# Attention and gated MoE on one core: a first chunk of four q-tiles, and the split of work between VectorE and GpSimd

## The chip, the cores and the metric

One core of a Trainium2 chip. The metric is the device time of one execution in microseconds. The kernel before took 841.29 us (median of three runs, 840.37 to 841.69). Engines are named as in the profile: PE is TensorE, DVE is VectorE, ACT is ScalarE, POOL is GpSimd, SP is SyncE, which issues most DMAs.

## What is computed

```python
def _attn_ref(q, k, v, n_sink, window):          # B, H, S, D = 4, 8, 768, 64; n_sink 4, window 128
   scores = scale * np.matmul(q, k.transpose(0, 1, 3, 2))
   rel = pos[:, None] - pos[None, :]
   keep = is_sink | ((rel >= 0) & (rel < window))
   scores = np.where(keep, scores, -1000000000.0)
   a = np.exp(scores - np.max(scores, axis=-1, keepdims=True))
   a = a / (np.sum(a, axis=-1, keepdims=True) + 1e-09)
   return np.matmul(a, v).astype(np.float32)

def _moe_ref(x, w_a, w_b, w_out):                # x 3072x512, w_a and w_b 512x1536, w_out 1536x512
   return ((x @ w_a) * (x @ w_b) @ w_out).astype(np.float32)
```

The attention's output, heads side by side, is x. The three weights come as float64.

## The kernel before

**Tiles and chunks.** A q-tile is 128 rows of one batch; there are 24. With a window of 128 and a few sink keys, q-tile t needs only key block t, block t - 1 and the sinks, so its scores are 128x264 (128x128 for t = 0, which has no block before it). The work goes in chunks of three q-tiles: `(b, t0, 3)` for pairs of batches, t0 = 0 and then 3. For each chunk there is an attention (8 heads x 3 tiles = 24 units) and then an MoE over the chunk's 384 rows.

**Stages.** `run` first does the attention of chunk 0 with nothing beside it (`alone=True`). Then, for each chunk, `moe` runs and the attention of the next chunk is drawn in beside it step by step: `attention` returns a generator, and `between(s)` takes as many of its steps as keep it evenly spread over the MoE's 36 thirds. The last chunk's MoE has no attention beside it.

**The MoE.** For each of 12 column blocks j: product a (`half("a", j)`), copied out by ACT as g (L670); product b, multiplied with g on DVE (L674); g is split into gh (ACT, L677) and gl (GpSimd, L679); then the output product of the block before (`project`, L662). Every float32 factor is used as an exact pair of parts, high and low (float32r), with three matmuls a product: 12 matmuls of n = 384 columns for a and for b, 9 of 512 columns for the output. PSUM banks: a, b, o0 to o2 for three outputs, and s, t, av for the attention.

**Weights.** Each of 36 weight tiles is loaded as float64 words and split on the core: two bit operations on DVE (L279, L284), a scaling of the low words on ACT (L283; on GpSimd for the first five, L281), a sum on GpSimd (L286), the high part on ACT (L293), and the low part on DVE (L298; on GpSimd for the first five). `weights_to` does one step of this pipeline: the bit operations of weight k, the high part of k - 3 (`D1`) and the low part of k - 4 (`D2`). These steps are taken from step 17 (`STEP0`) of the first attention on, at every second one (`STEPS`), and then once in each third of the first MoE. Loads run nine tiles ahead (`LOADS`).

**Attention.** The first two chunks use `parts_exact`, on float32 operands as they are; later ones use `parts_split`, with K, Q and V split into two parts by GpSimd (L326, L329). A unit: scores on PE; mask and maximum on DVE (L535); exp and sum on ACT (L537); two small DVE operations for the reciprocal (L539, L540); scaling of the probabilities, on DVE in the first attention (L542), on ACT in the others; transposes on PE (L564, L565) and a copy on ACT (L566); and once a head the product with V (L578). The transposes follow the scores by 3 units in the first attention and by 2 in the others. In the second attention K and Q of heads 3, 5 and 7 are split as in later ones (`SPLIT_KQ`).

**Order.** Each engine executes its instructions in order. The framework's planner chooses that order; instructions pinned with `keep_in_program_order` keep theirs among each other. Nearly all loads are on SP's queue, the outputs on ACT's (the last on SP's).

Of the kernel before, what the change touches and what calls it, by code (L numbers as in the profile page):

```python
# [19 lines left out]
P = 128  # L20
# [166 lines left out]
# Where a q-tile's transposed probabilities go (first slot, second slot, own block B before or after A),  # L187
# and the products of V with them: (key block, first slot, step of slots, first column tile). A lone slot
# (step 0) goes in with its two parts side by side, the low one's product into the fourth column tile.
UNITS = ((0, 4, "BA"), (1, 2, "AB"), (3, 5, "AB"))  # L190
GROUPS = ((0, 0, 1, 0), (2, 5, 0, 2), (-1, 4, 2, 0), (1, 2, 1, 1))


class Fast:
# [37 lines left out]
    def masks(self, val):  # L232
        """What is added to the scores: 0 where a key is kept, -NEG where it is not."""
# [37 lines left out]
    def early(self, kind, j):  # L271
        return 3 * j + "abo".index(kind) < POOL_FIRST

    def weight_bits(self, kind, j):
# [5 lines left out]
        if self.early(kind, j):  # L280
            nc.gpsimd.tensor_scalar(lo, lo.bitcast(U32), 2.0 ** -29, 1.0, op0=ALU.mult, op1=ALU.mult)  # L281
        else:
            pin(nc.scalar.activation(lo, lo.bitcast(U32), AF.Copy, scale=2.0 ** -29))  # L283
# [11 lines left out]
    def weight_low(self, kind, j):  # L295
        wh, wl = self.wt[kind, j]
        e = self.nc.gpsimd if self.early(kind, j) else self.nc.vector
        i = e.tensor_tensor(wl, self.wf.pop((kind, j)), wh.bitcast(F32), op=ALU.subtract)  # L298
# [73 lines left out]
    def attention(self, b, t0, nt, xf, exact=False, split=(), alone=False):  # L372
        parts = self.parts_exact(b, t0, nt, xf, split, alone) if exact else self.parts_split(b, t0, nt, xf)
# [107 lines left out]
    def parts_exact(self, b, t0, nt, xf, split, alone):  # L481
        """On float32 operands as they are (but K and Q of heads in `split`): more passes of the tensor engine."""
# [7 lines left out]
        preps, state, sc, vss, pts, skt = {}, {}, {}, {}, {}, {}  # L490

        def do_prep(h):
# [3 lines left out]
            if h in split:  # L496
                kq = self.prep_kq(b, h, t0, nt)
            else:
                if alone and h % 2:
                    k = self.io([P, MK], F32, f"kx{u}")  # L500
                else:
                    k = self.sp.tile([P, MK], F32, tag="ks", name=f"kx{u}")
                nc.sync.dma_start(k[:, :kw], self.kD[b, h, :, s0 * KB:s0 * KB + kw])
                q = self.sp.tile([P, 3 * P], F32, tag=("qh", "ql")[h % 2], name=f"qx{u}")
                nc.sync.dma_start(q[:, :nt * P], self.qT[b, h, :, t0 * P:(t0 + nt) * P])
                kq = k, q
            if h % 2 == 0:
                v = self.sp.tile([P, 2, 4, D], F32, tag="vv", name=f"vx{u}")
                nc.sync.dma_start(v[:, :, :nb], self.vB[b, h // 2, :, :, s0:s0 + nb])
            else:  # L510
                v = preps[h - 1][1]
            preps[h] = kq, v
            if h % 2 == 0 and late:
                vs = self.sp.tile([2 * NS, P], F32, tag="vs", name=f"vsx{u}")
                nc.sync.dma_start(vs, self.vS[b, h // 2, :2 * NS])
                vss[h // 2] = vs

        def scores(h, i):
            k, *qs = preps[h][0]
# [6 lines left out]
            for m, q in enumerate(qs):  # L526
                nc.tensor.matmul(ps[:, :w], lhsT=q[:, i * P:(i + 1) * P], rhs=k[:, c0:c0 + w],  # L527
                                 start=m == 0, stop=m == len(qs) - 1)
# [6 lines left out]
            nc.vector.tensor_tensor_reduce(out=p[:, :w], in0=ps[:, :w], in1=m, scale=-0.0625 * len(qs), scalar=BIG,  # L535
# [5 lines left out]
            if alone:  # L541
                nc.vector.tensor_scalar(p[:, :w], p[:, :w], st[:, 3:4], None, op0=ALU.mult)  # L542
# [3 lines left out]
            if i in late:  # L546
                if h % 2 == 0:
                    sc[h // 2, i] = self.at.tile([P, 2, NS], F32, tag=f"sc{i}", name=f"sc{u}", bufs=2)
                nc.vector.tensor_copy(sc[h // 2, i][:, h % 2, :], p[:, P:P + NS])

        def transposes(h, i):
# [5 lines left out]
            pt = pts[0][:, h % 2]  # L557
            n = units.index((h, i))
            tp = self.ps.tile([P, 2, P], F32, tag="tb"[n % 2] if alone else "t", name=f"t{u}")
            if t == 0:  # L560
                nc.tensor.transpose(tp[:, 1, :], p[:, :P], self.ident)
                nc.scalar.copy(pt[:, 1, :], tp[:, 1, :])
                return
            nc.tensor.transpose(tp[:, 0, :], p[:, :P], self.ident)  # L564
            nc.tensor.transpose(tp[:, 1, :], p[:, P + NS:], self.ident)  # L565
            nc.scalar.copy(pt[:, 2 * i:2 * i + 2, :], tp)  # L566

        def av(h):
            v = preps[h][1][:, h % 2]
            ps = self.ps.tile([P, 3 * P], F32, tag="av", name=f"av{tag}_{h}")  # L570
            rows = slice(0, D) if h % 2 == 0 else slice(D, P)
            pt = pts[0][:, h % 2]
            for i in range(nt):
                blks = [(t0 + i - s0, 2 * i + 1)]
                if t0 + i:
                    blks.append((t0 + i - 1 - s0, 2 * i))
                for k, (blk, sl) in enumerate(blks):
                    nc.tensor.matmul(ps[rows, i * P:(i + 1) * P], lhsT=v[:, blk, :], rhs=pt[:, sl, :],  # L578
                                     start=k == 0, stop=k == len(blks) - 1)
            nc.scalar.copy(xf[h // 2][rows, :nt * P], ps[rows, :nt * P])  # L580

        def sinks_t(pr):
            n = len(late)
            tp = self.ps.tile([2 * NS, 3 * P], F32, tag="t", name=f"skt{tag}_{pr}")
            for k, i in enumerate(late):
                nc.tensor.transpose(tp[:, k * P:(k + 1) * P], sc[pr, i].rearrange("p a b -> p (a b)"), self.ident)
            s = self.at.tile([2 * NS, 3 * P], F32, tag="sct", name=f"sct{tag}_{pr}", bufs=1)
            nc.vector.tensor_copy(s[:, :n * P], tp[:, :n * P])
            skt[pr] = s

        def sinks_av(pr):
            n = len(late)
            ps = self.ps.tile([P, 3 * P], F32, tag="av", name=f"sk{tag}_{pr}")
            nc.tensor.matmul(ps[:, :n * P], lhsT=vss[pr], rhs=skt.pop(pr)[:, :n * P], start=True, stop=True)
            xs = xf[pr][:, late[0] * P:nt * P]
            nc.vector.tensor_tensor(xs, ps[:, :n * P], xs, op=ALU.add)
# [3 lines left out]
    def pipeline(self, units, nt, late, do_prep, scores, transposes, av, sinks_t, sinks_av, lag):  # L600
        do_prep(0)
        yield
        nu = len(units)
        for k in range(nu + lag + 3):
            if k < nu:
                h, i = units[k]
                if i == 0:
                    do_prep(h + 1)
# [18 lines left out]
    def split_x(self, xf, nt, tag):  # L627
# [11 lines left out]
    def moe(self, row, nt, xf, between, weights_ahead, last):  # L639
# [26 lines left out]
        for j in range(NJ):  # L666
            weights_ahead(3 * j)
            pa = half("a", j)
            g = self.mo.tile([P, 3 * P], F32, tag="g", name=f"g{tag}_{j}", bufs=1)
# [5 lines left out]
            gh = self.mo.tile([P, 3 * P], F32R, tag="gh", name=f"gh{tag}_{j}")  # L675
            gl = self.mo.tile([P, 3 * P], F32R, tag="gl", name=f"gl{tag}_{j}")
# [19 lines left out]
    def run(self, scalars):  # L696
        chunks = [(b, t0, 3) for b0 in range(0, B, 2) for t0 in (0, 3) for b in (b0, b0 + 1)]
# [15 lines left out]
        xf = self.new_xf(0)  # L713
# [134 lines left out]
```

## Time and profile before

| | before |
|---|---|
| runs (us) | 841.69, 841.29, 840.37; median 841.29 |
| the profiled execution | span 839.9 us from the first to the last instruction |
| busy | PE 800.4 (95%), DVE 503.1 (60%), ACT 461.9 (55%), POOL 398.9 (47%) |
| first attention | 0 to about 44 us |
| first MoE chunk | about 44 to 174.5 us |
| six chunks with an attention of three tiles beside them | 98.7, 98.3, 93.9, 93.9, 98.5, 99.4 us |
| last chunk, and what follows it | 75.1 and 7.6 us |
| mean granted TensorE clock | 0.981 |

How to read the views: a row of stretches gives the stretch, its length, the busy time and number of instructions of each engine, the granted TensorE clock, the DMA engines' busy share and GB/s. A row of waits gives who waited for whom, the total, how often, and the longest. A row of a line gives its instructions with least, median and greatest duration in nanoseconds. A row of the timeline gives start and duration.

### The profile page before, as it was taken

What the parts mean: (1) busy time and instruction counts of PE and PEld (TensorE: products, weight loads), DVE (VectorE), ACT (ScalarE), POOL (GpSimd) and SP (SyncE); (2) the same over time, 40 slices, a digit from 0 to 9 for tenths busy, and PEclk for the clock granted to TensorE, in tenths of its full rate; (3) what the DMA queues carried; (4) which work ended last, traced back from release to release, by engine and by line L of the source; (5) the groups of instructions that cost most, each with busy time, mean ns of one, the idle gap of its engine ahead of it and who ended that gap; (6) DMA issues with size and microseconds to landing.
All of it is one profiled execution on the core that took longest, in us unless ns stands there. A gap on an engine that the chain in (4) does not pass through costs nothing.

```text
span 839.9 us, 13792 instructions
## 1 busy us (share of the span) xinstructions
PE 800.4 (95%) x4481; PEld 722.7 (86%) x4481; DVE 503.1 (60%) x1648; ACT 461.9 (55%) x1291; POOL 398.9 (47%) x493
## 2 busy tenths in 40 slices
PE   8977887999999999999999999999999999999996
PEld 5666776989998899999999999998999898999995
DVE  6999998555765576745656365646676567550101
ACT  5657666555554566645755466645665566542111
POOL 2375776835654365624555265624656346401110
PEclk9989999899999999999999999999999999999998
DMA  8944620321211133222333133321343113001001
GB/s 290 322 169 185 229 76 20 97 70 33 58 36 51 51 100 119 88 93 61 103 103 94 53 94 112 98 96 63 98 122 94 62 57 98 1 1 38 1 1 42
DMA packets 44977, 75.11 MB, mean 89 GB/s; under 512 B 4832, under 2 KB 25952, under 8 KB 44896
## 3 DMA queue, kind: packets, MB, share of 16 engines
q1 hardware_dynamic: 41840, 68.63, 25.9%
q10 hardware_dynamic: 3024, 5.51, 1.8%
q8 instruction: 37, 0.61, 0.3%
q14 instruction: 44, 0.36, 0.1%
q0 software_dynamic: 32, 0.00, 0.0%
HBM read 67.83 MB, written 6.29 MB: 88 GB/s over the span
## 4 chain that ended last, share of the span: by engine, by line
PE 77%; DVE 16%; ACT 4%; issue 2%; DMA 0%; ACTq 0%; DVEq 0%; POOLq 0%
PE o L662 22%; PE b L653 20%; PE a L653 20%; PE t L435 4%; PE av L451 4%; DVE sc L417 2%; PE s L399 2%; PE s L400 2%; DVE wf_b L279 1%; PE av L578 1%; DVE w_o L298 1%; DVE wf_a L279 1%; PE s L527 1%; DVE wf_b L284 1%; DVE wf_a L284 1%
## 5 line engine op out<-in xcount | busy, mean ns | idle before, releaser
L653 PE MATMUL a<-xh,w_a 128*128 128x384 f32 x768 | 221.4, 349 | 0.2 <-DVE st L535 0.2
L653 PE MATMUL b<-xh,w_b 128*128 128x384 f32 x768 | 218.3, 345 | 0.0
L679 POOL TENSOR_TENSOR gl<-g,gh 128x384 fp32r<-128x384 f32 x88 | 91.7, 1042 | 218.0 <-ACT gh L677 216.9
L662 PE MATMUL o<-w_o,gh 128*128 128x512 f32 x576 | 187.4, 407 | 0.0
L653 PEld LDWEIGHTS a<-xh,w_a 128*128 128x128 f32 x768 | 143.0, 192 | 2.2 <-DVE st L535 0.5
L653 PEld LDWEIGHTS b<-xh,w_b 128*128 128x128 f32 x768 | 141.1, 190 | 0.4 <-issue 0.2
L653 PE MATMUL a<-xl,w_a 128*128 128x384 f32 x384 | 131.0, 341 | 2.0 <-DVE xl L635 2.0
L653 PE MATMUL b<-xl,w_b 128*128 128x384 f32 x384 | 129.9, 338 | 0.0
L674 DVE TENSOR_TENSOR g<-b,g 128x384 f32<-128x384 f32 x96 | 53.1, 554 | 121.0 <-PE b L653 118.8
L662 PEld LDWEIGHTS o<-w_o,gh 128*128 128x128 f32 x576 | 104.1, 190 | 19.5 <-issue 0.7
L662 PE MATMUL o<-w_o,gl 128*128 128x512 f32 x288 | 114.3, 397 | 0.0
L670 ACT COPY g<-a 128x384 f32<-128x384 f32 x96 | 45.3, 472 | 89.6 <-PE a L653 86.3
L410 ACT ACTIVATE p<-p,st 128x264 f32<-128x264 f32 (+1 forms) x144 | 72.3, 502 | 40.2 <-DVE st L409 40.2
L677 ACT CAST gh<-g 128x384 fp32r<-128x384 f32 x96 | 49.3, 513 | 79.9 <-DVE g L674 79.6
L406 ACT ACTIVATE p<-p,st 128x264 f32<-128x264 f32 (+1 forms) x144 | 72.6, 504 | 33.1 <-DVE st L404 33.1
L653 PEld LDWEIGHTS a<-xl,w_a 128*128 128x128 f32 x384 | 73.9, 192 | 3.8 <-DVE xl L635 2.3
L653 PEld LDWEIGHTS b<-xl,w_b 128*128 128x128 f32 x384 | 73.3, 191 | 0.0
L417 DVE CAST sc<-p 128x16 fp32r<-128x16 f32 x112 | 54.3, 485 | 30.8 <-ACT p L410 29.5
L438 ACT CAST pt<-t 128x256 fp32r<-128x256 f32 (+1 forms) x144 | 51.2, 356 | 39.0 <-PE t L435 38.3
L439 DVE TENSOR_TENSOR pt<-t,pt 128x256 fp32r<-128x256 f32 (+1 forms) x144 | 58.0, 403 | 20.7 <-ACT pt L438 19.7
L404 DVE CUSTOM_DVE_ANT_0 p<-s,mg 128x264 f32<-128x264 f32 x112 | 47.7, 426 | 35.9 <-PE s L400 35.6
L326 POOL TENSOR_SCALAR qh<-qr 128x384 fp32r<-128x384 f32 x51 | 27.1, 531 | 88.1 <-PE s L399 63.9
(142 smaller groups left out, 1419.7 us busy)
## 6 DMA issues: line engine op xcount, KB each, us to landing
qr<-in_qT_dram SPq DMA_DIRECT2D x51, 192.0 KB, 2.4
raw_a<-in_wa_dram SPq DMA_DIRECT2D x12, 512.0 KB, 6.5
raw_b<-in_wb_dram SPq DMA_DIRECT2D x12, 512.0 KB, 6.6
raw_o<-in_wo_dram SPq DMA_DIRECT2D x12, 512.0 KB, 5.6
chk_a<-in_wa_dram SPq DMA_DIRECT2D x24, 256.0 KB, 2.7
chk_b<-in_wb_dram SPq DMA_DIRECT2D x24, 256.0 KB, 2.9
chk_o<-in_wo_dram SPq DMA_DIRECT2D x24, 256.0 KB, 2.8
out_dram<-os ACTq DMA_DIRECT2D x21, 256.0 KB, 2.1
```

What stands on the lines that cost most here:

```text
L404: nc.vector.tensor_tensor_reduce(out=p[:, :w], in0=ps[:, :w], in1=m, scale=-0.125, scalar=BIG, op0=ALU.add, op1=ALU.min, accum_out=st[:, 0:1])
L406: nc.scalar.activation(p[:, :w], p[:, :w], AF.Exp, bias=st[:, 0:1], scale=-1.0, accum_out=st[:, 1:2])
L410: nc.scalar.mul(p[:, :w], p[:, :w], st[:, 3:4])
L417: nc.vector.tensor_copy(c[:, :, 0, h % 2, :], sk)
L438: nc.scalar.copy(hs, tp[:, :n, :])
L439: nc.vector.tensor_tensor(ls, tp[:, :n, :], hs.bitcast(F32), op=ALU.subtract)
L653: nc.tensor.matmul(ps[:, :n], lhsT=w[:, ksl], rhs=x[:, :n], start=kk == 0 and i == 0, stop=kk == NK - 1 and i == 2)
L662: nc.tensor.matmul(outs[i], lhsT=g[:, sl], rhs=w, start=j == 0 and k == 0, stop=j == NJ - 1 and k == 2)
L670: nc.scalar.copy(g[:, :n], pa[:, :n])
L674: nc.vector.tensor_tensor(g[:, :n], pb[:, :n], g[:, :n], op=ALU.mult)
L677: nc.scalar.copy(gh[:, :n], g[:, :n])
L679: e.tensor_tensor(gl[:, :n], g[:, :n], gh[:, :n].bitcast(F32), op=ALU.subtract)
```

## The change

The chunks are now one of four q-tiles, one of the other two of the same batch, and six of three:

```diff
+CHUNKS = ((0, 0, 4), (0, 4, 2), (1, 0, 3), (2, 0, 3), (1, 3, 3), (2, 3, 3), (3, 0, 3), (3, 3, 3))
...
-        chunks = [(b, t0, 3) for b0 in range(0, B, 2) for t0 in (0, 3) for b in (b0, b0 + 1)]
+        chunks = CHUNKS
```

So the first attention has 32 units, the second (tiles 4 and 5 of batch 0) 16. The first MoE has 512 columns, the second 256; the fourth output of the first takes the bank av, so the second attention shares one bank between transposes and products (`half_bank`). The outputs are staged in the buffers of gh and gl instead of three of their own:

```diff
+        def half_bank(second, name):
+            if not bank:
+                bank[0] = self.ps.tile([P, 4, P], F32, tag="t", name=name)
+            return bank[0][:, 2:] if second else bank[0][:, :2]
...
-        outs = [self.ps.tile([P, DM], F32, tag=f"o{i}", name=f"o{tag}_{i}") for i in range(nt)]
+        outs = [self.ps.tile([P, DM], F32, tag=("o0", "o1", "o2", "av")[i], name=f"o{tag}_{i}") for i in range(nt)]
...
-            o = self.mo.tile([P, DM], F32, tag="os", bufs=3, name=f"os{tag}_{i}")
+            o = self.mo.tile([P, DM], F32, tag=("gh", "gl")[i % 2], name=f"os{tag}_{i}")
```

In the first attention the probabilities are scaled, and the sink columns copied, on GpSimd instead of DVE. K, Q and V are loaded two heads ahead instead of one, Q of every head into a buffer of its own; x of the first chunk lies in buffers of late weights:

```diff
             if alone:
-                nc.vector.tensor_scalar(p[:, :w], p[:, :w], st[:, 3:4], None, op0=ALU.mult)
+                nc.gpsimd.tensor_scalar(p[:, :w], p[:, :w], st[:, 3:4], None, op0=ALU.mult)
...
-                nc.vector.tensor_copy(sc[h // 2, i][:, h % 2, :], p[:, P:P + NS])
+                (nc.gpsimd if alone else nc.vector).tensor_copy(sc[h // 2, i][:, h % 2, :], p[:, P:P + NS])
...
-        return self.pipeline(units, nt, late, *parts, 3 if alone else 2)
+        return self.pipeline(units, nt, late, *parts, *((3, 2) if alone else (2, 1)))
...
+                q = self.mo.tile([P, nt * P], F32, tag=f"x{'hl'[h % 2]}{h // 2}", name=f"qx{u}", bufs=1)
...
+        pairs = [self.wp.tile([P, 2, nt * P], F32, tag=f"w_{k}{NJ - 1}", name=f"xf0_{k}") for k in "bo"]
+        xf = [x[:, i, :] for x in pairs for i in range(2)]
```

The low part of every third weight (all of w_b) is made on GpSimd, the others on DVE; the low words of the first five are scaled on ACT like the rest. Splitting begins at step 15 of the first attention. `SPLIT_KQ` is gone, so all heads of the second attention are on float32 as they are:

```diff
-POOL_FIRST = 5
-STEP0, STEPS = 17, 2
+POOL_LOW = (1, 3)
+STEP0, STEPS = 15, 2
...
-    def early(self, kind, j):
-        return 3 * j + "abo".index(kind) < POOL_FIRST
+    def low_engine(self, kind, j):
+        return self.nc.gpsimd if (3 * j + "abo".index(kind)) % POOL_LOW[1] == POOL_LOW[0] else self.nc.vector
...
-        if self.early(kind, j):
-            nc.gpsimd.tensor_scalar(lo, lo.bitcast(U32), 2.0 ** -29, 1.0, op0=ALU.mult, op1=ALU.mult)
-        else:
-            pin(nc.scalar.activation(lo, lo.bitcast(U32), AF.Copy, scale=2.0 ** -29))
+        pin(nc.scalar.activation(lo, lo.bitcast(U32), AF.Copy, scale=2.0 ** -29))
...
-        e = self.nc.gpsimd if self.early(kind, j) else self.nc.vector
+        e = self.low_engine(kind, j)
...
-SPLIT_KQ = (3, 5, 7)
```

More of the change, by code (lines that the diff above doesn't have):

```diff
@@ L370, in prep_v, with attention @@
         return vv
[L372 to L373 removed]
+    def attention(self, b, t0, nt, xf, exact=False, alone=False):
+        parts = self.parts_exact(b, t0, nt, xf, alone) if exact else self.parts_split(b, t0, nt, xf)
         late = [i for i in range(nt) if t0 + i >= 2]
         units = [(h, i) for h in range(H) for i in range(nt)]
[L376 removed]
+        return self.pipeline(units, nt, late, *parts, *((3, 2) if alone else (2, 1)))
     def parts_split(self, b, t0, nt, xf):
@@ L479, in parts_split, with parts_exact @@
         return do_prep, scores, transposes, av, sinks_t, sinks_av
-    def parts_exact(self, b, t0, nt, xf, split, alone):
+    def parts_exact(self, b, t0, nt, xf, alone):
         nc = self.nc
@@ L556, in transposes @@
                 pts[0] = self.cp.tile([P, 2, 7, P], F32, tag="pt", name=f"ptx{u}")
-            pt = pts[0][:, h % 2]
             n = units.index((h, i))
[L559 to L566, printed above, removed]
-        def av(h):
-            v = preps[h][1][:, h % 2]
-            ps = self.ps.tile([P, 3 * P], F32, tag="av", name=f"av{tag}_{h}")
+            if alone:
+                tp = self.ps.tile([P, 2, P], F32, tag="tb"[n % 2], name=f"t{u}")
+            else:
+                tp = half_bank(0, f"t{u}")
+            k = max(2 * i - (t0 == 0), 0)
+            parts = [p[:, :P]] if t == 0 else [p[:, :P], p[:, P + NS:]]
+            for m, part in enumerate(parts):
+                nc.tensor.transpose(tp[:, m, :], part, self.ident)
+            nc.scalar.copy(pts[0][:, h % 2, k:k + len(parts), :], tp[:, :len(parts), :])
+        def av(h):
+            v = preps[h][2][:, h % 2]
+            if alone:
+                ps = self.ps.tile([P, 4, P], F32, tag="av", name=f"av{tag}_{h}")
+            else:
+                ps = half_bank(1, f"av{tag}_{h}")
             rows = slice(0, D) if h % 2 == 0 else slice(D, P)
@@ L573, in av @@
             for i in range(nt):
-                blks = [(t0 + i - s0, 2 * i + 1)]
+                k = 2 * i - (t0 == 0)
+                blks = [(t0 + i - s0, k + 1)]
                 if t0 + i:
[L576 to L580, printed above, removed]
+                    blks.append((t0 + i - 1 - s0, k))
+                for m, (blk, sl) in enumerate(blks):
+                    nc.tensor.matmul(ps[rows, i, :], lhsT=v[:, blk, :], rhs=pt[:, sl, :],
+                                     start=m == 0, stop=m == len(blks) - 1)
+            nc.scalar.copy(xf[h // 2][rows, :nt * P].rearrange("p (c q) -> p c q", q=P), ps[rows, :nt, :])
         def sinks_t(pr):
             n = len(late)
-            tp = self.ps.tile([2 * NS, 3 * P], F32, tag="t", name=f"skt{tag}_{pr}")
+            if alone:
+                tp = self.ps.tile([P, 4, P], F32, tag="t", name=f"skt{tag}_{pr}")
+            else:
+                tp = half_bank(0, f"skt{tag}_{pr}")
             for k, i in enumerate(late):
-                nc.tensor.transpose(tp[:, k * P:(k + 1) * P], sc[pr, i].rearrange("p a b -> p (a b)"), self.ident)
+                nc.tensor.transpose(tp[:2 * NS, k, :], sc[pr, i].rearrange("p a b -> p (a b)"), self.ident)
             s = self.at.tile([2 * NS, 3 * P], F32, tag="sct", name=f"sct{tag}_{pr}", bufs=1)
-            nc.vector.tensor_copy(s[:, :n * P], tp[:, :n * P])
+            nc.vector.tensor_copy(s[:, :n * P].rearrange("p (c q) -> p c q", q=P), tp[:2 * NS, :n, :])
             skt[pr] = s
@@ L592, in sinks_av, with pipeline @@
             n = len(late)
[L593 to L596, printed above, removed]
+            if alone:
+                ps = self.ps.tile([P, 4, P], F32, tag="av", name=f"sk{tag}_{pr}")
+            else:
+                ps = half_bank(1, f"sk{tag}_{pr}")
+            nc.tensor.matmul(ps[:, :n, :], lhsT=vss[pr], rhs=skt.pop(pr)[:, :n * P], start=True, stop=True)
+            xs = xf[pr][:, late[0] * P:nt * P].rearrange("p (c q) -> p c q", q=P)
+            nc.vector.tensor_tensor(xs, ps[:, :n, :], xs, op=ALU.add)
         return do_prep, scores, transposes, av, sinks_t, sinks_av
-    def pipeline(self, units, nt, late, do_prep, scores, transposes, av, sinks_t, sinks_av, lag):
-        do_prep(0)
+    def pipeline(self, units, nt, late, do_prep, scores, transposes, av, sinks_t, sinks_av, lag, early):
+        for h in range(early):
+            do_prep(h)
         yield
@@ L607, in pipeline @@
                 if i == 0:
-                    do_prep(h + 1)
+                    do_prep(h + early)
                 scores(h, i)
@@ L668, in moe @@
             pa = half("a", j)
-            g = self.mo.tile([P, 3 * P], F32, tag="g", name=f"g{tag}_{j}", bufs=1)
+            g = self.mo.tile([P, max(n, 3 * P)], F32, tag="g", name=f"g{tag}_{j}", bufs=1)
             nc.scalar.copy(g[:, :n], pa[:, :n])
@@ L725, in run @@
                 nxf = self.new_xf(c + 1)
-                gen = self.attention(nb, nt0, nnt, nxf, exact=c == 0, split=SPLIT_KQ)
+                gen = self.attention(nb, nt0, nnt, nxf, exact=c == 0)
                 steps = H * nnt + 5
```

52 lines of the change are left out of this document (23 added, 29 removed).

## The prediction

> **What bounds the kernel now.** I read the page's first part, then the busy time by stretches, then what TensorE waited for, then single lines. The stretches are cut where the chain of work shows stages to begin: weights start to be split at 27.4 us, the first attention ends near 44, the last weight part is written at 162.4, the first MoE chunk ends at 174.5, and the later cuts are chunk ends.
>
> ```profile
> span 839.9 us, 13792 instructions
> PE 800.4 (95%) x4481; PEld 722.7 (86%) x4481; DVE 503.1 (60%) x1648; ACT 461.9 (55%) x1291; POOL 398.9 (47%) x493
> ```
>
> ```profile
> core 0: us, PE busy (x) PEld busy (x) DVE busy (x) ACT busy (x) POOL busy (x), PEclk, DMA share, GB/s
> 0.00:6.40 6.40, 4.89 (x12) 2.14 (x12) 1.94 (x10) 1.28 (x1) 2.13 (x11) 1.00 0.65 166
> 6.40:27.40 21.00, 19.86 (x105) 13.72 (x105) 16.82 (x99) 14.45 (x53) 3.51 (x5) 0.92 0.92 323
> 27.40:44.00 16.60, 14.94 (x80) 10.13 (x78) 16.50 (x53) 10.64 (x34) 7.93 (x6) 0.90 0.99 350
> 44.00:162.40 118.40, 100.27 (x508) 86.48 (x507) 106.69 (x218) 76.31 (x188) 83.85 (x65) 0.91 0.35 122
> 162.40:174.50 12.10, 12.10 (x65) 10.17 (x64) 4.39 (x10) 5.02 (x11) 5.94 (x10) 1.00 0.40 120
> 174.50:273.20 98.70, 96.60 (x566) 89.51 (x565) 60.11 (x205) 53.20 (x140) 50.65 (x67) 1.00 0.17 49
> 273.20:371.50 98.30, 96.60 (x566) 89.32 (x565) 62.12 (x221) 59.59 (x172) 49.56 (x67) 1.00 0.29 88
> 371.50:465.40 93.90, 93.11 (x534) 86.22 (x533) 51.02 (x189) 55.72 (x172) 46.09 (x67) 1.00 0.29 89
> ...
> 559.30:657.80 98.50, 96.81 (x567) 89.32 (x566) 64.04 (x221) 59.67 (x172) 50.77 (x67) 1.00 0.30 91
> 657.80:757.20 99.40, 96.70 (x566) 89.36 (x566) 60.10 (x222) 56.42 (x156) 39.97 (x51) 1.00 0.15 44
> 757.20:832.30 75.10, 75.09 (x396) 69.89 (x394) 7.93 (x14) 13.24 (x27) 11.20 (x11) 1.00 0.03 11
> 832.30:839.90 7.60, 0.27 (x1) 0.08 (x1) 0.30 (x2) 0.58 (x1) 0.00 (x0) 0.70 0.33 115
> ```
>
> From 174.5 us on TensorE is busy without gaps at a granted clock of 1.00; what counts there is only its work. The last chunk has no attention beside it: 75.1 us for three q-tiles, 25.03 a tile. So attention costs 18.8 us of TensorE where it is for tiles 0 to 2 (93.9 - 75.1) and 23 to 24 for tiles 3 to 5.
>
> The loss is before 162.4. DVE is busy 16.50 of 16.60 us and 106.69 of 118.40, and TensorE at a clock of 0.90 to 0.91 waits for it:
>
> ```profile
> PE s L527 <- DVE st L535: 8.0, 8, 2.6
> PE t L561 <- DVE st L539: 6.4, 2, 4.2
> ```
>
> But DVE's busy time is itself mostly waiting. The same scaling (L542) takes 0.35 us with GpSimd idle and 1.33 us when a GpSimd add begins just ahead of it:
>
> ```profile
> 27.80 0.35 DVE L542 TENSOR_SCALAR p<-p,st 128x264 f32<-128x264 f32 x1
> ...
> 32.77 1.28 POOL L286 TENSOR_TENSOR wf_b<-wf_b,raw_b 128x512 int32<-128x512 int32 x1 [2.58 <-DVE st L540]
> 32.88 0.08 DVE L535 DVE_READ_ACCUMULATOR2_ANT st<- 128x1 f32 x1
> 32.88 1.33 DVE L542 TENSOR_SCALAR p<-p,st 128x264 f32<-128x264 f32 x1
> ```
>
> The lines by minimum, median and maximum (ns) say which operations are hit: those that work from SBUF to SBUF. The product from PSUM (L674) never moves.
>
> ```profile
> L279 DVE TENSOR_SCALAR wf_b<-raw_b x12: 414/1341/1543, 31.5 to 147.0; 128x512 int32<-128x512 int32 x12
> L284 DVE SCALAR_TENSOR_TENSOR wf_b<-raw_b,wf_b x12: 681/693/1694, 31.9 to 148.4; 128x512 int32<-128x512 int32 x12
> L298 DVE TENSOR_TENSOR w_b<-wf_b,w_b x10: 670/692/1672, 64.4 to 159.1; 128x512 fp32r<-128x512 f32 x10
> L298 POOL TENSOR_TENSOR w_a<-wf_a,w_a x2: 1273/1492/1711, 35.9 to 48.7; 128x512 fp32r<-128x512 f32 x2
> L286 POOL TENSOR_TENSOR wf_b<-wf_b,raw_b x12: 1279/1363/2287, 32.8 to 150.6; 128x512 int32<-128x512 int32 x12
> L674 DVE TENSOR_TENSOR g<-b,g x96: 539/557/560, 54.2 to 828.2; 128x384 f32<-128x384 f32 x96
> L679 POOL TENSOR_TENSOR gl<-g,gh x88: 996/1014/1507, 57.5 to 823.1; 128x384 fp32r<-128x384 f32 x88
> L326 POOL TENSOR_SCALAR qh<-qr x51: 502/512/836, 87.7 to 719.6; 128x384 fp32r<-128x384 f32 x51
> L326 POOL TENSOR_SCALAR vv<-vr x48: 344/403/725, 162.6 to 731.1; 128x256 fp32r<-128x256 f32 x32, 128x192 fp32r<-128x192 f32 x16
> ```
>
> So I count such DVE operations and all GpSimd ones as one queue, each at its undisturbed time. In 44 to 162.4 the same view by single lines counts, for L279, L284, L298, L286, L326 and L329 in turn:
>
> ```profile
> 44.00:162.40 118.40, 28.19 (x31) 0.91 0.35 122
> 44.00:162.40 118.40, 30.93 (x32) 0.91 0.35 122
> 44.00:162.40 118.40, 29.51 (x31) 4.91 (x3) 0.91 0.35 122
> 44.00:162.40 118.40, 47.24 (x32) 0.91 0.35 122
> 44.00:162.40 118.40, 7.59 (x10) 0.91 0.35 122
> 44.00:162.40 118.40, 12.16 (x10) 0.91 0.35 122
> ```
>
> That is 31 x 0.41 + 32 x 0.68 + 31 x 0.68 + 3 x 1.27 + 32 x 1.29 = 100.7 us, and some 24 more for ten low parts of g (1.0 each), the parts of K, Q and V (the last two rows, 19.8 with their waits, about 13 without) and small copies: 125 in 118.4 us, a ratio of 1.055. The queue of the two engines, not DVE alone, sets the pace of this stage.
>
> [...]
>
> **The change, part by part.** Times are the profile's (span 839.9; the page does not say which run it is; the runs' median is 841.29, so 1.4 us lie outside).
>
> *Later chunks.* After the first chunk the rest is TensorE's work, by the rows above: the two-tile chunk 50.1 + 18.8 = 68.9 (its companion is now tiles 0 to 2 of batch 1), then 93.9, 98.3, 98.5, 93.9 and 99.4, the last 75.1 and the tail 7.6: 635.6, against 665.4 before. That saves 29.8. In the two-tile chunk a unit of attention comes every 68.9 / 29 = 2.4 us instead of 3.3. Its cover for GpSimd's low part of g shrinks from two steps of 2.6 us to two of 1.9, while a head's K, Q and V parts take about 4 us of GpSimd in a row. I add 2.5 us; bounds 0 and 16 (2 us at each of eight heads).
>
> *First attention up to the weights.* Before, 17 steps take 21.0 us, 1.235 each. A head has 7 key blocks on 4 tiles instead of 5 on 3, so a step costs 5% more, 1.30; splitting starts at step 15. Loads are a third larger, about 0.5 us to the first one: 6.4 + 0.5 + 19.5 = 26.4. The extra 1.3 MB of K, Q and V is 3.8 us of DMA at 350 GB/s, on SP's queue among weight loads that run eight weights ahead and now two heads ahead: taken at nothing, 3.8 at most.
>
> *First attention with the weights.* Now 12 weights are begun here (every second step from 15 to 37), not 7, with 8 low parts. Queue: 12 x (0.41 + 0.68 + 1.29) = 28.6; low parts 5 x 0.68 + 3 x 1.27 = 7.2; scaling of 17 units on GpSimd 6.4; copies and x parts 3.7. Together 45.9, at 1.055 43.5, of which the last round falls into the MoE: 40 us. TensorE alone would need 23 x 1.30 = 30. The scaling's price on GpSimd with a factor per partition isn't in the trace. I take 0.41, by the L326 row (0.403 for 128x256), the nearest form; the bounds are 0.34, that row's least, and 0.70, a two-input form (1.0 for 384 columns, L679) scaled to 264. DVE is rid of 17 x 0.35 = 6 us for it; so against my 40 the unknown is worth -6 (if DVE's relief counts in full) to +5 us. It puts GpSimd's queue, with adds of 1.3 us, into the chain from scores to transposes, which has three steps of slack (4 to 5 us); late next is the transpose. Before, the first and the seventh weight were begun 14 steps apart, at 1.36 us a step:
>
> ```profile
> 27.48 0.41 DVE L279 TENSOR_SCALAR wf_a<-raw_a 128x512 int32<-128x512 int32 x1
> ...
> 46.47 1.12 DVE L279 TENSOR_SCALAR wf_a<-raw_a 128x512 int32<-128x512 int32 x1
> ```
>
> ```profile
> L283 ACT ACTIVATE raw_a<-raw_a 128x512 int32<-128x512 uint32 x10 | 6.7, 668 | 0.0
> ```
>
> Mine is 1.74, for 46 us of queue where the same count gives some 22 there. ACT takes the first five weights' conversions (0.67 each) from GpSimd: 3.4 us, under the queue while ACT has room (10.64 of 16.60 before). The attention ends at 66.4, against 44.
>
> *First MoE chunk.* Four tiles: 100.1 us of TensorE. Beside it 16 units of tiles 4 and 5, 32 key blocks on float32: at most 0.74 a block (1.235 over 1.67 blocks), at least 0.49 (23.6 over 48, the split form); I take 22 us, near the upper end as these are also float32. That is 122, 3.4 a step. The queue has 24 weights x 2.38 = 57, low parts 19 x 0.68 + 9 x 1.27 = 24, nine low parts of g at 1.33 = 12, small ones 5: 98, 93 us at the old ratio, while TensorE's 28 steps are 95. With both full I take 100, then eight steps at 3.4 without weights: 127. The K and Q parts of three heads (9 us of the queue) are gone. Leaving the first five weights' conversion and low part to GpSimd cost the queue some 6 us, which are saved; a third of the low parts there costs 12 x 0.59 = 7, so the two cancel. The chunk ends at 193.4 instead of 174.5.
>
> *Off the path:* outputs staged in the buffers of g's parts must have landed (row below) before the next chunk's first part is written, after its first a and b products, 2.8 us or more; the first output is copied over 1 us before the chunk ends, so this costs nothing, or 1 us a chunk at the slowest landing. The bank that transposes and products share in the second attention held one tile of each before as well: nothing; a wait of 0.4 us for a copy in each of 16 units, 6 us, if TensorE had no MoE product to put between.
>
> ```profile
> DMA to landing us min/median/max: 2.0/2.1/3.5
> ```
>
> Sum: 193.4 + 2.5 + 635.6 = 831.5 in the profile, 8.4 less; as a median 833.
>
> **Rivals.** (1) *TensorE's own pace.* Steps of the attention run at 1.45 us (33 us), since DVE no longer holds the scaling, and the MoE takes 123: 26.4 + 33 + 123 + 638 = 820, about 822. For it: the 16.8 of 21 us of DVE before the weights; against it the ratio of 1.055.
> (2) *The queue of the two engines stops the attention (slower).* Scores, GpSimd scaling and DVE's weight operations block each other in turn, each step waiting for an add. At 2.2 us a step (mine and a third of an add; 50 us) and 131 for the MoE the sum is 26.4 + 50 + 131 + 638 = 845, about 847. It decides above 2.1 us a step, where the 8.4 us are gone. For it: waits up to 4.2 us on DVE already; against it: 1.36 us a step before with the same weights. [...]
> (3) *The two-tile chunk starves on GpSimd:* up to 16 us instead of 2.5: 845, about 846. Against it: TensorE's waits after 174.5 are 2 us a chunk.
>
> **How the numbers follow.** My sum 0.52 (own range 826 to 840), rival 1 0.24, rival 2 0.16, rival 3 0.08. A difference under 0.2% (1.7 us) can't be told from none. Faster: 0.24 and most of 0.52, 0.69; same 0.06; slower 0.25. The range reaches from a little under rival 1 (816) to rivals 2 and 3 (848).
>
> **What would show it.** The last product of the first attention near 66 us; the first chunk's end near 193 with a clock near 1.00 from 70 us on; weights finished near 165 to 170, earlier than the chunk by eight steps; the two-tile chunk in 69 to 74 us. I am wrong if steps with weights take over 2 us, if GpSimd's scaling takes over 0.7, or if the two-tile chunk shows TensorE waiting for gl.

## The result, and the profile after

The changed kernel took 849.9 us (median of four runs, 849.08 to 853.03) against 841.49 (840.37 to 842.26) for the kernel before: a ratio of 1.0109, 95% interval 1.0087 to 1.0132. It is slower; 833.0 with a range to 848 was forecast. The first lines of the page of the changed kernel:

```profile
span 847.3 us, 13814 instructions
...
PE 804.9 (95%) x4481; PEld 705.0 (83%) x4481; DVE 472.8 (56%) x1585; ACT 460.6 (54%) x1288; POOL 418.0 (49%) x531
```

The work has moved as the change says: DVE is busy 30 us less than before, GpSimd 19 us more. By stretches, cut where the weights begin, where the first attention ends (its last product starts at 70.6 us), where TensorE's long gaps end (114), once more inside the first chunk (162), where that chunk ends, and at the ends of the two-tile chunk and of the last one:

```profile
core 0: us, PE busy (x) PEld busy (x) DVE busy (x) ACT busy (x) POOL busy (x), PEclk, DMA share, GB/s
0.00:23.90 23.90, 18.68 (x95) 11.43 (x96) 12.55 (x77) 13.69 (x45) 13.87 (x30) 1.00 0.82 286
23.90:71.00 47.10, 35.70 (x165) 21.54 (x163) 30.40 (x100) 27.71 (x80) 40.58 (x43) 0.80 0.67 245
71.00:114.00 43.00, 36.58 (x149) 27.09 (x149) 36.04 (x65) 25.55 (x54) 27.49 (x19) 0.94 0.48 174
114.00:162.00 48.00, 47.32 (x222) 35.74 (x221) 39.13 (x83) 31.28 (x70) 30.69 (x23) 1.00 0.19 52
162.00:207.50 45.50, 45.50 (x211) 35.08 (x211) 12.79 (x34) 15.93 (x37) 16.49 (x21) 1.00 0.15 42
207.50:280.20 72.70, 69.93 (x497) 63.47 (x497) 46.78 (x173) 45.81 (x139) 42.76 (x67) 1.00 0.20 60
...
762.00:837.20 75.20, 75.17 (x397) 69.96 (x395) 7.93 (x14) 13.26 (x27) 11.21 (x11) 1.00 0.03 11
837.20:847.30 10.10, 0.27 (x1) 0.08 (x1) 0.28 (x2) 0.58 (x1) 0.00 (x0) 0.66 0.26 89
```

The first chunk ends at 207.5 us, 33.0 later than before (174.5); from there to the last product it takes 629.7 us instead of 657.8, 28.1 less; and what follows is 2.5 longer. So the shape gave back nearly what I had counted (29.8), and all of the loss but those 2.5 us lies ahead of 207.5. There DVE is no longer the busy engine: between 23.9 and 71 it is busy 30.40 of 47.10 us, GpSimd 40.58, TensorE at a granted clock of 0.80.

The scaling on GpSimd, with who waited for it:

```profile
L543 POOL TENSOR_SCALAR p<-p,st x32: 602/942/1635, 8.4 to 65.2; 128x264 f32<-128x264 f32 x24, 128x128 f32<-128x128 f32 x8
...
who waited for it (us, times):
  PEld t L566: 17.9, 16
  PE t L566: 11.8, 12
  DVE p L536: 8.9, 10
```

One takes 0.94 us for 128x264 (0.60 for 128x128), where I took 0.41 and at most 0.70. In the stretch with the weights 20 of them fill 20.96 us, in the same view for that line alone:

```profile
23.90:71.00 47.10, 20.96 (x20) 0.80 0.67 245
```

What it does to the others is seen in order of time, GpSimd's instructions first, then DVE's (in brackets the idle time ahead of an instruction, and what ended it):

```profile
42.03 1.27 POOL L297 TENSOR_TENSOR w_b<-wf_b,w_b 128x512 fp32r<-128x512 f32 x1
43.27 1.46 POOL L285 TENSOR_TENSOR wf_b<-wf_b,raw_b 128x512 int32<-128x512 int32 x1
44.71 0.94 POOL L543 TENSOR_SCALAR p<-p,st 128x264 f32<-128x264 f32 x1
...
46.92 1.29 POOL L285 TENSOR_TENSOR wf_o<-wf_o,raw_o 128x512 int32<-128x512 int32 x1 [0.44 <-ACT ptx L567]
```

```profile
42.62 0.96 DVE L281 TENSOR_SCALAR wf_o<-raw_o 128x512 int32<-128x512 int32 x1
45.68 0.43 DVE L536 CUSTOM_DVE_ANT_0 p<-s,mg 128x264 f32<-128x264 f32 x1 [2.09 <-POOL p L543]
46.04 0.08 DVE L536 DVE_READ_ACCUMULATOR2_ANT st<- 128x1 f32 x1
46.04 0.74 DVE L283 SCALAR_TENSOR_TENSOR wf_o<-raw_o,wf_o 128x512 int32<-128x512 int32 x1
```

The scaling at 44.71 stood behind a low part and a sum of the weights. DVE's next mask waits 2.09 us and starts as it ends; behind the mask, on DVE in order, stands L283 (46.04 to 46.78; the result of L281 that it takes was done at 43.58), which makes what GpSimd's next sum (L285, from 46.92) adds up. So a late scaling delays DVE's weight work too. The other way round the waits are small: in this stage GpSimd waited for DVE 3.5 us by the profile (2.2 for a reciprocal, 1.3 for L283 at the stage's end), and the 0.44 us here are put down to ACT. What waits most are TensorE's transposes (L566), for the scaling on GpSimd.

### The profile page after: what moved, and what is told of

It reads as the page before. It is cut to its first block, busy times and chain, and to the rows that moved or that the text cites. A ratio compares the mean times of both kernels' runs of the same rounds, so it can differ in the third digit from the quotient of the medians.

```text
span 847.3 us, 13814 instructions
## 1 busy us (share of the span) xinstructions
PE 804.9 (95%) x4481; PEld 705.0 (83%) x4481; DVE 472.8 (56%) x1585; ACT 460.6 (54%) x1288; POOL 418.0 (49%) x531
## 4 chain that ended last, share of the span: by engine, by line
PE 80%; DVE 9%; ACT 3%; POOL 3%; issue 2%; DMA 2%; SPq 0%; POOLq 0%; ACTq 0%; DVEq 0%
PE o L674 22%; PE b L665 21%; PE a L665 20%; PE t L434 4%; PE av L450 3%; PE s L398 2%; PE s L399 2%; POOL p L543 2%; PE s L529 2%; DVE sc L416 1%; PE av L583 1%; PE t L566 1%; PE t L583 1%; ACT p L405 1%; DVE sc L417 1%
## 5 line engine op out<-in xcount | busy, mean ns | idle before, releaser
L665 PE MATMUL b<-xh,w_b 128*128 128x384 f32 (+2 forms) x768 | 217.6, 345 | 0.0
L665 PE MATMUL a<-xh,w_a 128*128 128x384 f32 (+2 forms) x768 | 216.4, 343 | 0.0
L691 POOL TENSOR_TENSOR gl<-g,gh 128x384 fp32r<-128x384 f32 (+2 forms) x88 | 90.8, 1031 | 211.0 <-ACT gh L689 193.0
L665 PE MATMUL a<-xl,w_a 128*128 128x384 f32 (+2 forms) x384 | 129.5, 337 | 1.2 <-DVE xl L647 1.2
L665 PE MATMUL b<-xl,w_b 128*128 128x384 f32 (+2 forms) x384 | 130.0, 338 | 0.0
L686 DVE TENSOR_TENSOR g<-b,g 128x384 f32<-128x384 f32 (+2 forms) x96 | 53.1, 554 | 128.2 <-PE b L665 125.7
L409 ACT ACTIVATE p<-p,st 128x128 f32<-128x128 f32 (+1 forms) x144 | 71.4, 496 | 38.0 <-DVE st L408 38.0
L405 ACT ACTIVATE p<-p,st 128x128 f32<-128x128 f32 (+1 forms) x144 | 71.6, 497 | 34.8 <-DVE st L403 34.6
L438 DVE TENSOR_TENSOR pt<-t,pt 128x128 fp32r<-128x128 f32 (+1 forms) x144 | 56.9, 395 | 21.4 <-ACT pt L437 20.1
L325 POOL TENSOR_SCALAR qh<-qr 128x384 fp32r<-128x384 f32 x48 | 24.8, 517 | 84.8 <-PE s L398 59.9
L674 PEld LDWEIGHTS o<-w_o,gl 128*128 128x128 f32 x288 | 54.1, 188 | 13.6 <-POOL gl L691 0.5
L434 PE MATMUL t<-ident,p 128*128 128x128 f32 x264 | 54.1, 279 | 6.3 <-DVE pt L438 5.8
```

The source lines that it names most:

```text
L405: nc.scalar.activation(p[:, :w], p[:, :w], AF.Exp, bias=st[:, 0:1], scale=-1.0, accum_out=st[:, 1:2])
L409: nc.scalar.mul(p[:, :w], p[:, :w], st[:, 3:4])
L434: nc.tensor.transpose(tp[:, k, :], parts[o], self.ident)
L438: nc.vector.tensor_tensor(ls, tp[:, :n, :], hs.bitcast(F32), op=ALU.subtract)
L665: nc.tensor.matmul(ps[:, :n], lhsT=w[:, ksl], rhs=x[:, :n], start=kk == 0 and i == 0, stop=kk == NK - 1 and i == 2)
L674: nc.tensor.matmul(outs[i], lhsT=g[:, sl], rhs=w, start=j == 0 and k == 0, stop=j == NJ - 1 and k == 2)
```

## Experiments

In all of them that have the new shape the time from the end of the first chunk on is the same within 3.1 us (637.2 to 640.3), so what differs beyond that lies in the first attention and the first chunk. The kernel before, run beside them, had medians of 840.4 to 841.5. The stages by the profiles (us), as cut at the first split weight, the last product of the first attention and the last output product of the first chunk:

| kernel | weights begin | attention ends | first chunk | median |
|---|---|---|---|---|
| changed | 23.9 | 71.0 | 136.5 | 849.9 |
| scaling on DVE | 24.0 | 61.0 | 136.4 | 837.2 |
| low parts on DVE | 25.1 | 66.9 | 135.4 | 844.2 |
| both on DVE | 25.3 | 60.5 | 135.8 | 835.6 |
| GpSimd, constants | 23.3 | 58.7 | 136.5 | 837.0 |
| GpSimd, two tensors | 22.5 | 64.2 | 136.4 | 844.1 |
| changed, slower pace | 24.4 | 70.6 | 133.6 | 846.8 |
| both on DVE, slower pace | 24.8 | 60.4 | 133.0 | 833.4 |
| the same, from step 11 | 20.6 | 64.9 | 133.3 | 837.4 |
| the same, half on ACT | 23.7 | 56.3 | 132.9 | 828.8 |
| the same, all on ACT | 23.8 | 57.0 | 131.4 | 830.6 |

"First chunk" is the length of that chunk. "The same" in the third last row is the kernel with both on DVE and the slower pace, but with splitting from step 11; the last two have it from step 15 again.

**Scaling back on DVE.**

```diff
-                nc.gpsimd.tensor_scalar(p[:, :w], p[:, :w], st[:, 3:4], None, op0=ALU.mult)
+                nc.vector.tensor_scalar(p[:, :w], p[:, :w], st[:, 3:4], None, op0=ALU.mult)
...
-                (nc.gpsimd if alone else nc.vector).tensor_copy(sc[h // 2, i][:, h % 2, :], p[:, P:P + NS])
+                nc.vector.tensor_copy(sc[h // 2, i][:, h % 2, :], p[:, P:P + NS])
```

> The changed kernel with the scaling of the probabilities and the copy of the sink columns of the first attention back on VectorE; all else as changed. Theory A (the price: 0.94 us a scaling on GpSimd, against 0.41 that I took, fills the queue that VectorE and GpSimd share): 20 scalings stand between 24 and 71 us, each 0.59 us cheaper, 12 us of queue or 11 us of time; the first attention ends near 60 to 62, the first chunk near 196 to 199, the time is 838 to 841. Rival B (the shape: a longer attention with nothing beside it and twelve weights begun under it, whoever scales): VectorE takes back 0.35 us a unit and is held up as before; the time is 847 to 852.

837.18 us, ratio to before 0.9951 (0.9933 to 0.9969), a little under the range of theory A, whose stages came as said (61.0 and 197.4). The two lines of the change that were undone cost 12.7 us, and the rest of it made the kernel faster. In the stretches of this kernel the stage with the weights is 10 us shorter; another 2.4 of the 12.7 lie behind the last output product (see the last section):

```profile
24.00:61.00 37.00, 32.07 (x152) 19.86 (x151) 34.80 (x122) 27.34 (x78) 16.09 (x12) 0.86 0.81 300
```

DVE is full here (34.80 of 37.00) and still the stage is faster than with GpSimd at 40.58 of 47.10. The first MoE chunk is as long as before, 136.4.

**All low parts on DVE.**

```diff
-        return self.nc.gpsimd if (3 * j + "abo".index(kind)) % POOL_LOW[1] == POOL_LOW[0] else self.nc.vector
+        return self.nc.vector
```

> The changed kernel with all low weight parts on VectorE (none on GpSimd); the scaling stays on GpSimd. By the shared queue each of twelve parts is 0.59 us cheaper, 7 us in all, of which those before 114 us (seven, 4 us) count: 845 to 847. Rival: the parts held VectorE free for the attention's chain, then it is slower, 851 to 855. Without any part on the path: 849 to 851.

844.18 us, 1.0048 (1.0023 to 1.0072): 5.7 less than the changed kernel, a little more than expected. By the profiles 4.1 of it lie before the attention's end, where GpSimd then has less ahead of each scaling.

**Both,** the two edits together.

> Both moves undone together: scaling, sink copies and all low parts on VectorE, chunks of four, two and three tiles as changed. Theory A: the sum of the two, 834 to 838, which is below the kernel before (841). Rival B: no better than 846.

835.61 us, 0.9942 (0.992 to 0.9964), in the range of theory A. But the two gains do not add up (12.7 and 5.7, together 14.3): with the scaling gone from GpSimd, a low part there holds up little, and the 1.6 us between this run and the one with the scaling alone undone are within the intervals. What is left of the change, the shape, the loads, the earlier start of splitting and the low words on ACT, is worth 5.7 us.

**Scaling alone moved, in the kernel before.** The copy (L549) is left on DVE.

```diff
-                nc.vector.tensor_scalar(p[:, :w], p[:, :w], st[:, 3:4], None, op0=ALU.mult)
+                nc.gpsimd.tensor_scalar(p[:, :w], p[:, :w], st[:, 3:4], None, op0=ALU.mult)
```

> The kernel before with only the scaling of the first attention moved to GpSimd. Theory A: of 24 scalings 9 fall beside weight splitting, 5 us of queue; the others delay the transposes a little; 845 to 849. Rival B: it relieves VectorE, the engine that is busy all the time there: 836 to 841.

855.85 us, 1.019 (1.0161 to 1.0219): the sign was right, the size wrong, 14.5 us instead of 4 to 8. GpSimd's instructions in order of time show a cost that I had overlooked:

```profile
2.95 0.24 POOL L223 IOTA col<- 128x128 f32 x1
13.00 0.64 POOL L281 TENSOR_SCALAR raw_a<-raw_a 128x512 int32<-128x512 uint32 x1 [9.81 <-DMA raw_a<-in_wa_dram]
13.73 1.54 POOL L542 TENSOR_SCALAR p<-p,st 128x128 f32<-128x128 f32 x2
```

and its waits another (from 0 to 56 us):

```profile
DVE sc L549 <- POOL p L542: 11.1, 8, 3.3
...
PEld t L561 <- POOL p L542: 9.1, 3, 6.1
```

Here the first scalings stand behind the scaling of a weight's low words, which waits 9.81 us for its load, and DVE's copies wait 11.1 us for GpSimd with masks behind them. So this run held three things at once, and I took two of them out.

**The same, without the two waits.** Copies on GpSimd as well, and the low words of all weights on ACT, as in the changed kernel:

```diff
-        if self.early(kind, j):
-            nc.gpsimd.tensor_scalar(lo, lo.bitcast(U32), 2.0 ** -29, 1.0, op0=ALU.mult, op1=ALU.mult)
-        else:
-            pin(nc.scalar.activation(lo, lo.bitcast(U32), AF.Copy, scale=2.0 ** -29))
+        pin(nc.scalar.activation(lo, lo.bitcast(U32), AF.Copy, scale=2.0 ** -29))
```

> The kernel before with scaling and copies of the first attention on GpSimd, and the low words of the first five weights scaled on ACT. With only the scaling moved it took 855.9, 14.5 us more; its first scaling stood on GpSimd's queue behind the scaling of the first weight's low words, which waited 9.8 us for that weight's load. Theory A: 8 to 10 of the 14.5 us were that wait and the copies on DVE that waited for GpSimd (11.1 us), and what is left is the price of the scaling: 845 to 849. Rival B: the price alone makes 14 us, 853 to 857.

845.22 us, 1.0052 (1.0036 to 1.0069), in theory A's range, and both waits are gone from the trace: the first scaling starts at 9.3 us instead of 13.7. The two edits took away 10.8 of the 14.5 us; 3.7 are left for 24 scalings in the old shape. How the 10.8 divide between the two waits was not tried. So without two other parts of the change, low words on ACT and copies on GpSimd, the scaling on GpSimd would have cost far more.

**The price by itself: constants.** The factor is left out, the step stays where it is.

```diff
-                nc.gpsimd.tensor_scalar(p[:, :w], p[:, :w], st[:, 3:4], None, op0=ALU.mult)
+                nc.gpsimd.tensor_scalar(p[:, :w], p[:, :w], 1.0, 1.0, op0=ALU.mult, op1=ALU.mult)
```

> The changed kernel, but the probabilities of the first attention are multiplied on GpSimd by two constants instead of by a factor per partition, so the normalisation is left out; where and when the step runs stays. Theory A (price): the row of L543 falls from 0.94 to about 0.40 us for 128x264, as in the nearest form with constants. In the 47 us between the first split weight and the end of the first attention, 20 scalings then take 11 us less of the queue of the two engines, so that stage ends near 61 instead of 71 and the run takes 838 to 842. Rival B (place): it is GpSimd's queue in the chain from scores to transposes that costs the time, whatever one scaling takes; then the run stays at 846 to 850. If the row itself stays above 0.7, the form with constants is not the cheaper one and the run tells nothing of A against B.

837.03 us, 0.9948 (0.9927 to 0.9968). The line now reads:

```profile
L543 POOL TENSOR_SCALAR p<-p x32: 290/410/855, 7.8 to 54.5; 128x264 f32<-128x264 f32 x24, 128x128 f32<-128x128 f32 x8
```

0.41 us, the very price I had taken, and the run is level with the one that scales on DVE (837.0 and 837.2). The stage with the weights takes 35.40 us:

```profile
23.30:58.70 35.40, 29.12 (x160) 18.00 (x159) 31.97 (x100) 27.05 (x80) 31.38 (x41) 0.97 0.86 327
```

Rival B, that the place costs the time whatever the price, falls; and as the copies stay on GpSimd here, they cost little. One thing is not kept apart: the step no longer reads the reciprocal from DVE. In the changed kernel the scaling waited 3.0 us for it in all (four times), so by estimate it accounts for a small part of the 12.9 us at most; the next run reads it again.

**The price by itself: two tensors.**

```diff
+                nc.gpsimd.tensor_tensor(p[:, :w], p[:, :w], st[:, 3:4].to_broadcast([P, w]), op=ALU.mult)
```

> The changed kernel, with the scaling on GpSimd as a product of two tensors (the factor read as a column repeated over the row) instead of a tensor and a factor per partition. By the two-input row of L691 (1.30 us for 512 columns, 1.00 for 384) one takes about 0.70 for 128x264 instead of 0.94. Theory A (the time follows the price on the shared queue): 20 scalings take 5 us less in the first attention, which ends near 66, and the run takes 843 to 846, between the 837.0 at 0.41 and the 849.9 at 0.94. Rival B (only a form with constants is cheap): the row stays at 0.9 or above and the run at 848 to 851.

844.05 us, 1.0036 (1.0021 to 1.0051), as theory A has it; the row:

```profile
L543 POOL TENSOR_TENSOR p<-p,st x32: 394/628/1247, 8.3 to 58.9; 128x264 f32<-128x264 f32 x24, 128x128 f32<-128x128 f32 x8
```

It computes the same as the changed kernel, factor and all; its scaling waited 2.2 us for the reciprocal. At 0.41, 0.63 and 0.94 us a scaling the attention ends at 58.7, 64.2 and 71.0 and the runs take 837.0, 844.1 and 849.9: the time follows the price. It does not follow in proportion (7.0 us for the first 0.22 us, 5.9 for the next 0.31); why is not shown.

**A slower pace of weights.** What TensorE loses in the first chunk it loses in about the chunk's first 43 us (after that at most 0.7 us, in the ten kernels of the new shape whose stretches were cut there). There a score waits while DVE works through weights (DVE's instructions of the changed kernel, and the waits on TensorE's side in 71 to 114):

```profile
92.70 1.18 DVE L283 SCALAR_TENSOR_TENSOR wf_b<-raw_b,wf_b 128x512 int32<-128x512 int32 x1
93.81 0.41 DVE L281 TENSOR_SCALAR wf_o<-raw_o 128x512 int32<-128x512 int32 x1
94.25 1.66 DVE L283 SCALAR_TENSOR_TENSOR wf_o<-raw_o,wf_o 128x512 int32<-128x512 int32 x1
95.83 0.42 DVE L536 CUSTOM_DVE_ANT_0 p<-s,mg 128x264 f32<-128x264 f32 x1
```

```profile
PE s L529 <- DVE st L536: 3.7, 2, 3.5
PE t L566 <- ACT xf L585: 1.4, 1, 1.4
PE a L665 <- DVE xl L647: 1.2, 2, 0.7
```

```diff
-                weights_to(max(s + AHEAD, done[0] + 1 - D2), LOADS)
+                weights_to(s + AHEAD if s % 4 == 3 else max(s + AHEAD, done[0] + 1 - D2), LOADS)
```

> The changed kernel, but in the first MoE chunk a weight is begun in three of four thirds instead of in every third until they are done. In the changed kernel and in the two with scaling on DVE alike, TensorE loses 11 to 13 us in the first 43 us of that chunk and nothing after. Theory A (the weights are begun faster than the chunk needs them, so DVE's in-order queue holds the masks and scores back): the loss falls with the pace, by 4 to 9 us: 841 to 846. Rival B (the loss has another source, such as x arriving late or a weight loaded late): no change within 2 us, 848 to 852. Rival C: the weights come too late at the end of the chunk, slower than 852.

846.76 us, 1.0077 (1.0047 to 1.0107): 3.1 less, under the 4 to 9 of theory A and more than rival B allows. The interval overlaps that of the changed kernel, so the time alone does not show a gain; in the profile the chunk is 2.9 us shorter (133.6). The stretches of its first part:

```profile
70.60:114.00 43.40, 38.72 (x159) 29.09 (x160) 34.05 (x63) 25.90 (x57) 25.10 (x18) 0.94 0.54 193
114.00:204.20 90.20, 90.00 (x420) 68.90 (x419) 56.13 (x116) 46.88 (x104) 49.51 (x44) 1.00 0.15 45
```

TensorE is busy 38.72 us instead of 36.58, but gaps and a clock of 0.94 remain, and so does the wait of scores for masks that theory A blamed (3.4 us instead of 3.7). So the pace is some 3 of the loss, not all of it, and not by the mechanism that I had in mind.

The same edit in the kernel with scaling and low parts on DVE:

> Scaling and all low parts on DVE, with a weight begun in three of four thirds of the first MoE chunk. By theory A as above 827 to 832 against 835.6 without the slower pace; by rival B 834 to 838; by rival C above 838.

833.37 us, 0.9909 (0.988 to 0.9938), above the 827 to 832 of theory A; the chunk is 133.0 instead of 135.8. The same small gain; here too the intervals overlap. The wait of scores for masks falls from 3.8 to 0.3 us, but that of transposes for a copy on ACT grows from 1.0 to 3.5: the gap moves more than it goes.

**Earlier weights,** in that last kernel:

```diff
-STEP0, STEPS = 15, 2
+STEP0, STEPS = 11, 2
```

> Scaling and low parts on DVE, weights begun in three of four thirds of the first chunk, and splitting from step 11 of the first attention instead of 15, so two more weights are begun there. Theory A: the shared queue has room before the weights (DVE 16.5 of 25 us busy, GpSimd 2), so two weights (4.8 us of queue) leave the MoE's first thirds, where TensorE still loses 8 us: 830 to 832.5 against 833.4. Rival B: the loads are late there (DMA engines 0.86 busy), DVE waits for a weight with the masks queued behind it: 834 to 838.

837.35 us, 0.9948 (0.9928 to 0.9967): slower than with step 15 (the intervals just touch), so theory A falls. The time is in rival B's range, but not by its mechanism, since DVE waits for no weight load there (4.1 us in all from 14 to 65 us, all for TensorE). Its stage with the weights:

```profile
20.60:64.90 44.30, 35.15 (x181) 22.06 (x182) 42.21 (x151) 32.30 (x91) 14.90 (x11) 0.96 0.76 278
```

DVE is busy 42.21 of 44.30 us. The attention ends 4.5 us later, about what two more weights of queue would take (2 x 2.4), and the chunk behind it is no shorter (133.3): two weights fewer in it do not help.

**Scaling on ACT for every second unit** from unit 15 on, otherwise as with step 15:

```diff
-            if alone:
+            if alone and (n < STEP0 or n % 2 == 0):
                 nc.vector.tensor_scalar(p[:, :w], p[:, :w], st[:, 3:4], None, op0=ALU.mult)
             else:
                 nc.scalar.mul(p[:, :w], p[:, :w], st[:, 3:4])
```

> The same kernel with splitting from step 15, but from unit 15 of the first attention on every second scaling is on ACT. DVE is busy 34.7 of 35.6 us there, ACT 27.3. Theory A: eight scalings leave the shared queue, at 0.35 to 1.3 us each: 3 to 5 us less in that stage, 829 to 832. Rival B: ACT, with the conversions of the weights queued in front of the exponentials, takes the place of DVE: 833.4 or more.

828.75 us, 0.9854 (0.9833 to 0.9875): 4.6 us less than with all on DVE and faster than both kernels, as theory A had it. The stage takes 32.60 us, with DVE at 30.49 and ACT at 29.11:

```profile
23.70:56.30 32.60, 27.43 (x145) 17.21 (x144) 30.49 (x116) 29.11 (x84) 11.86 (x10) 0.95 0.87 319
```

With all scalings from unit 15 on ACT:

```diff
-            if alone and (n < STEP0 or n % 2 == 0):
+            if alone and n < STEP0:
```

> As the kernel with every second scaling on ACT (828.75 us), but from unit 15 of the first attention on all of them are on ACT. Theory A (the shared queue of DVE and GpSimd is still what that stage waits for): eight or nine more scalings leave it, 826 to 828. Rival B: ACT is busy 30.7 of 34.2 us already; with some 4.5 us more it is full, and exponentials and scalings wait for each other: 829 to 834.

830.57 us, 0.9884 (0.9865 to 0.9903): in rival B's range, but the intervals overlap, so it can't be told from the half. ACT is busy 30.82 of 32.00 us there (24 to 56).

## Why the prediction was wrong

**The step that failed first: the price of the scaling.** I had no row of a GpSimd operation with a factor per partition, took the form with constants as nearest (0.41) and set 0.70 as the upper bound, from the two-input form. The form with a factor took 0.94, outside both bounds. The stage with the weights took 47.1 us (2.05 a step) instead of 40 (1.74). That it is the price and not the placing is shown by the run with constants (35.4 us), with the run of two tensors between (41.7). Had I put 0.94 in, 17 scalings x 0.53 / 1.055 make 8.5 us more, 48.5: the sum would have stood at 840.0 in the profile, no faster than before (839.9).

**The step that failed second: the first MoE chunk,** 136.5 us instead of 127, wherever the scaling stood (135.4 to 136.5 in six kernels). It has two parts. TensorE's need was 122; by the stretch almost without gaps (222 + 211 instructions in 93.50 us, 0.216 each) the chunk's 582 are 126, so by this estimate the attention beside it costs 26, not 22, or 0.81 us a key block: I had held 0.74 for the upper end. And I spread 98 us of queue evenly over 28 steps and found it just hidden, at a loss of 5; the loss was 10.8, all before 114 us: TensorE stood idle 6.4 us there (43.00 - 36.58), nearly all in the three waits shown above, and its 149 instructions took 0.246 us each, 4.4 more than at 0.216, at a clock of 0.94. Some 3 of the 10.8 go with the pace at which weights are begun (seen in two profiles, with the times' intervals overlapping). The rest, about 8, I have only seen: masks, copies and x's parts waited for, and a clock of 0.88 to 0.95 in that part of the new-shape kernels. It did not go when two weights were taken out. Its cause stays open.

**The sum of the error.** Against the profiled execution I was 15.8 us short (847.3 for 831.5): -2.5 for the start of the weights (23.9, not 26.4), +7.1 for the stage, +9.5 for the chunk, +1.3 for the two-tile chunk (72.7, not 71.4), -2.1 for the other chunks, +2.5 for the tail. In the kernel with constants, priced as I had it, the first chunk ends at 195.2 against my 193.4; the sum there is near by luck, from errors that cancel: a start 3.1 us too late, a stage 4.6 too long and a chunk 9.5 too short.

**Two readings that were wrong.** I wrote that DVE's busy time is mostly waiting. By the rows beside it, L279, L284 and L298 took 88.6 us on DVE where 55.6 would be undisturbed: 33 of 106.69 us, a third. And the seven weights of the kernel before are begun at every second step, so the first and the seventh are 12 steps apart, not 14: 19.0 us make 1.58 us a step, not 1.36, much nearer to the 1.74 of my sum.

**What held.** The two-tile chunk came in its 69 to 74 us, and TensorE's matmuls wait there for nothing of GpSimd's (no such row among the waits from 207.5 to 280.2), so rival 3 is out. The weights were finished at 175.0, later than my 165 to 170, but nine to ten steps ahead of the chunk's end (I had eight). The later chunks are TensorE's work (busy 620.86 of the 629.7 us from 207.5 on). The queue that the two engines share is borne out in the main: a scaling at 0.41 on GpSimd and one at 0.35 on DVE end in the same time (837.0 and 837.2), though the stages differ by 1.6 us (35.4 and 37.0) and the longer tail on GpSimd's side hides it. One queue is a reading of these times (before, 0.35 us against 1.33 for the same scaling on DVE); why the two engines hold each other up is not shown.

**Which rival happened.** Rival 2, in its place and in most of its mechanism: transposes waiting for GpSimd (17.9 and 11.8 us by the rows above), DVE's masks waiting too (8.9). But it came only through the price: with constants the same queue, adds and all, let the attention go at 1.54 us a step. Its 847 lies near the 849.9 partly by luck, from a longer stage (50 us for 47.1) and a shorter chunk (131 for 136.5). I gave it 0.16 and set its point of decision at 2.1 us a step; at 2.05 the kernel was already slower, because the chunk was longer than I had it, wherever the scaling stood. Against it I had held the old pace of weights, which had no scaling on GpSimd in it, so it was no evidence. Nor does a scaling in the queue of the two engines set this rival apart: it had its place there on DVE as well (0.35 to 1.33 us).

## What to carry to other kernels

Before work is moved to another engine, find a row of that very form there, operands and all, and if there is none, let the upper bound be wider than the nearest forms say; the price of a form decided some 13 us here. Ask what stands ahead of the moved instruction in its new queue and what it waits for: a step in a chain between two engines must not stand behind one that waits for a load (9.81 us in one run here), and the reader of its result must not stand in front of what feeds it (DVE's copies waited 11.1 us). An engine beside the crowded pair (ACT here) can be worth a part of such work though one step is dearer there: a scaling took 0.52 us on ACT and 0.36 on DVE (medians), and yet every second one moved was worth 4.6 us; all of them, with ACT busy 30.82 of 32.00 us, no more.

## What the runs showed of the hardware

The same multiplication on GpSimd, 128x128 and 128x264 float32, took 0.29 and 0.41 us with constants, 0.39 and 0.63 as a product of two tensors, and 0.60 and 0.94 with a factor per partition (least and median of the rows above): 0.9, 1.7 and 2.5 ns for each of the 136 columns between. I had not expected the last to be dearer than two whole tensors; why it is, is not shown.

What follows the last output product was longer in five kernels, the changed one and four of its variants with GpSimd's scaling: 9.7 to 10.9 us from the issue of the last outputs to the end, against 8.2 to 8.6 in the other nine. So some 2 us of their times lie there. GpSimd has 519 to 531 instructions in them; in the two variants of the kernel before with scaling on GpSimd (517 and 520) the end was not longer, so the number alone does not explain it. The cause is not settled.
